# Attention scores as three float32r products on row halves, in an attention + MoE kernel

## The chip, the cores and the metric

The kernel runs on one core of a Trainium2 chip. The metric is the device time of one execution in microseconds. The engines are TensorE (PE, with its weight loads shown apart as PEld), VectorE (DVE), ScalarE (ACT), GpSimd (POOL) and SyncE (SP), which here issues the DMAs.

## The reference, cut to what matters

Attention with a learned bias by relative position comes first, with 4 batches, 8 heads, 576 tokens and 64 dimensions a head. Its output goes through a dense feed-forward layer (512 to 2048 to 512, 2304 tokens) and then a soft mixture of eight experts.

```python
scores = scale * np.matmul(q, k.transpose(0, 1, 3, 2))
...
h = np.maximum(x @ w1 + b1, 0.0)      # x: psi_rel / psi_i
bias = h @ w2
scores = scores + bias.transpose(2, 0, 1)[None, :, :, :]
scores = scores - np.max(scores, axis=-1, keepdims=True)
attn = np.exp(scores)
attn = attn / (np.sum(attn, axis=-1, keepdims=True) + 1e-09)
return np.matmul(attn, v).astype(np.float32)
...
h = x @ w_in
g = np.maximum(h, 0.0) + alpha * np.minimum(h, 0.0)
return (g @ w_out).astype(np.float32)
```

q and k are drawn large (factors 22 and 8), so the scores need nearly full float32.

## The kernel before, in words

**Stages.** The bias phase (0 to about 76 us) builds the bias with TensorE from masks that VectorE, ScalarE and GpSimd make, and stores its rows (`rows`) in a DRAM scratch `W`, from which the tiles `nb` are loaded. Attention follows (76 to about 395 us), then the feed-forward layer, called MoE in the code (to about 850), and the experts.

**Attention.** Work goes by 16 pairs: four head pairs `hp` times four batches. A pair has nine tiles of 128 query rows (`SLOT` gives their order; slots 0 to 3 and 5 to 8 are whole tiles of one head, slot 4 has the last 64 rows of both heads). `run` goes over the steps (pair i, tile t). A step issues:

- `scores` of the tile four steps ahead (L348): the 64 dimensions of a head stand twice in `raw`, on partitions 0 to 63 and 64 to 127, and each half multiplies the same queries with one half of the keys (288 columns), in float32. VectorE drains both halves from PSUM, adds the bias and takes the row's extreme (z and m, L353); ScalarE takes the exponential (e, L364).
- `transposes` of the tile of this step (L382): ten per tile, five chunks on either row half into two PSUM tiles, which ScalarE (L391) and VectorE (L393) copy into `g`.
- `sums` once a pair: reciprocals, and their transpose `tr` (L417), copied to `rt` (L419).
- `pv` (L402) when four or nine tiles are done: ten float32 matmuls of 256 or 320 columns into one PSUM tile `o`, which ScalarE copies to `xo` (L406) and a DMA stores in `xT`.

The input `raw` of a pair (q, k and v) is loaded two pairs ahead, in three buffers.

**Order.** The code order above is not the order on the engines: a planner moves instructions on their engine's queue, except those handed to `keep_in_program_order`. It decides from its own estimates, for instance, between which transposes a PV matmul stands, and where in VectorE's queue the MoE's first operations stand: `x_sum` (L504) multiplies loaded attention output (`xa` or `stage`) with its loaded row factors `rb`. Waits of DMAs are in SP's queue order: what SP's queue holds behind a waiting DMA waits too. `load_alpha` loads `nal` and lets GpSimd negate it.

PSUM holds two score tiles, three transpose tiles and one `o`. In the MoE, weights and activations are split in two float32r parts, and each product is three float32r products (`w0h`, `w0l`: the parts of the weights, the second made by GpSimd at L556).

Of the kernel before, what the change touches and what calls it, by code (L numbers as in the profile page):

```python
# [8 lines left out]
F32 = mybir.dt.float32  # L9
F32R = mybir.dt.float32r  # L10
# [3 lines left out]
AF = mybir.ActivationFunctionType  # L14
ALU = mybir.AluOpType
# [53 lines left out]
def bias_phase(tc, ident, W, cpack, lcol, prow, xmain, xtail, att):  # L69


    nc = tc.nc
    with ExitStack() as ctx:
# [162 lines left out]
        for k in range(NG):  # L236
            cs = [c for c in range(3, -1, -1) if k <= NG - 1 - c]
            if k < 5:
                cs.append(4)
            done = 0  # L240
            for n_, c in enumerate(cs):
                unit(k, c)
                if c in (2, 3) and k + c == 8:
                    att.bias_first(3 - c)
                if k + 1 < NG:
                    upto = 16 * (n_ + 1) // len(cs)
                    for u in range(done, upto):
# [9 lines left out]
class Attention:  # L257
# [7 lines left out]

    DONE = {3: 0, 8: 1}

    def __init__(self, tc, ident, W, xT, rs, qkv):
        self.tc, self.nc, self.ident = tc, tc.nc, ident
        self.W, self.xT, self.rs = W, xT, rs  # L270
        self.qkv = qkv
# [43 lines left out]
    def load(self, i):  # L315
        nc = self.nc
        hp, b = self.pairs[i]
        if b == 0 and hp > 0:
            self.bias_tile(hp)
            self.bias_rows(hp, 0, 4)  # L320
            self.bias_rows(hp, 4, 1)
        raw = self.rp.tile([P, 2368], F32, tag="raw", name=f"raw{i}")
        ins = nc.sync.dma_start(raw, self.qkv[hp, b])
        if i == 3:
            self.tc.keep_in_program_order(ins)
        self.st[i] = dict(
            hp=hp,
            b=b,
            i=i,
            q=raw[:, :1152].rearrange("p (h n) -> p h n", h=2),  # L330
            k=raw[:, 1152:1728].rearrange("p (h n) -> p h n", h=2),
            v=raw[:, 1728:].rearrange("p (h c d) -> p h c d", h=2, d=D),
        )

    def scores(self, i, t):
        nc, st = self.nc, self.st[i]
        slot = self.SLOT[t]
        if slot == 0:
            st["sum"] = self.op.tile([P, 9], F32, tag="sum", name=f"sum{i}")
        s = self.ps_s.tile([P, 2, 512], F32, tag="s", name=f"s{i}_{t}")  # L340
        if slot == 4:
            terms = [(64 * h, 64, h, 512) for h in range(2)]
        else:
            terms = [(0, P, slot // 5, P * (slot % 5))]
        for o, m_, h, r0 in terms:
            for hf in range(2):
                d = slice(64 * hf, 64 * hf + 64)
                nc.tensor.matmul(  # L348
                    s[o : o + m_, hf, :288], st["q"][d, h, r0 : r0 + m_], st["k"][d, h], start=True, stop=True
                )  # L350
        z = self.zp.tile([P, S], F32, tag="z", name=f"z{i}_{t}")
        m = self.zp.tile([P, 1], F32, tag="m", name=f"m{i}_{t}")
        nc.vector.tensor_tensor_reduce(  # L353
            out=z.rearrange("p (a b) -> p a b", a=2),
            in0=s[:, :, :288],
            in1=self.nb[st["hp"]][:, slot].rearrange("p (a b) -> p a b", a=2),
            scale=-0.125,
            scalar=3.0e38,
            op0=ALU.add,
            op1=ALU.min,  # L360
            accum_out=m,
        )
# [9 lines left out]
    def transposes(self, i, t):  # L372

        nc, st = self.nc, self.st[i]
        slot = self.SLOT[t]
        e = st.pop(("e", t))
        tp = [self.ps_t.tile([P, 5, 64], F32, tag="t", name=f"t{i}_{t}_{r}") for r in range(2)]
        for c in range(5):
            for r in range(2):
                q = slice(64 * r, 64 * r + 64)  # L380
                k0 = min(P * c, S - P)
                nc.tensor.transpose(tp[r][:, c], e[q, k0 : k0 + P], self.ident[q, q])  # L382
        for r in range(2):
            if slot == 4:
                dst = self.g_tile(st, r, 1)[:, :, 256:]
# [6 lines left out]
            else:  # L392
                nc.vector.tensor_copy(dst, tp[r])  # L393

    def pv(self, i, half):
        nc, st = self.nc, self.st[i]
        g = [st.pop(("g", h, half)) for h in range(2)]
        n = 320 if half else 256
        o = self.ps_o.tile([P, 320], F32, tag="o", name=f"o{i}_{half}")
        for c in range(5):  # L400
            for h in range(2):
                nc.tensor.matmul(  # L402
                    o[64 * h : 64 * h + 64, :n], st["v"][:, h, c], g[h][:, c, :n], start=c == 0, stop=c == 4
                )
        xo = self.op.tile([P, 320], F32, tag="xo", name=f"xo{i}_{half}")
        nc.scalar.activation(xo[:, :n], o[:, :n], AF.Copy)  # L406
        c0 = st["b"] * S + 256 * half
        nc.sync.dma_start(self.xT[st["hp"], :, c0 : c0 + n], xo[:, :n])

    def sums(self, i):  # L410
# [6 lines left out]
        nc.tensor.transpose(tp[:9], r, self.ident)  # L417
# [587 lines left out]

@with_exitstack
def kernel(
    ctx, tc, qkv, cpack, w_l, alpha, phi, mw1, mw2, lcol, prow, xmain, xtail, scon, out
):
    nc = tc.nc  # L1010
    dram = ctx.enter_context(tc.tile_pool(name="scratch", bufs=1, space=DRAM))
# [4 lines left out]
    ident = const.tile([P, P], F32, name="ident")  # L1016
    make_identity(nc, ident)

    att = Attention(tc, ident, W, xT, rs, qkv)
    att.open_set(ctx, 0)  # L1020
    rctx = ExitStack()
    att.rp = rctx.enter_context(tc.tile_pool(name="a_raw", bufs=3, reuse_waits="tile", side="right"))
# [107 lines left out]
def _layout(i):  # L1130
# [9 lines left out]
    parts = [np.stack([q, q], axis=2), kh, v_l]  # L1140
    qkv = np.concatenate([a.reshape(HP, B, P, -1) for a in parts], axis=3)
    wi = i["moe_w_in"].view(np.int64).reshape(NC, P, NF, P).transpose(2, 1, 0, 3).reshape(NF, P, NC * P)
    wo = i["moe_w_out"].view(np.int64).reshape(NF, P, DM)
    return dict(
        qkv=qkv,
        cpack=np.concatenate(
            [
                np.tile(i["w1"].reshape(HID, 1), (4, 1)),
# [41 lines left out]
```

## Time and profile before

| what | us |
|---|---|
| median of 3 runs | 934.61 (931.73 to 934.78) |
| the profiled execution | 929.26 |
| its span from first to last instruction | 927.4 |

| stage (us from the span's start) | what runs |
|---|---|
| 0 to 76 | bias phase |
| 76 to 395 | attention, 16 pairs |
| 395 to 850 | MoE |
| 850 to 927 | experts |

The profile is one execution. Its rows give an instruction group's source line, engine, operation, output and inputs with shapes and count; a float32 matmul leaves several records. "Idle before" is the time an engine stood still just before the group, with what released it. The granted clock is a share of full speed: 1.00 is 2.4 GHz, and 0.5 is 1.2 GHz.

### The profile page before, as it was taken

The page shows a single profiled execution, that of the slowest core. Times are in us where ns is not written, and L with a number is a line of the kernel's source. Part 1 is how long each engine was busy: PE and PEld are TensorE (multiplying, and loading weights), DVE is VectorE, ACT ScalarE, POOL GpSimd, SP SyncE. Part 2 cuts the span into 40 slices and gives each one's busy share as a digit, 9 for nine tenths or more (in the row PEclk, how much of TensorE's full clock was granted, in tenths as well). Part 3 has the DMA queues.
Part 4 walks back from the last instruction along what each step waited for, and adds up shares of the span by engine and source line. Part 5 has one row for each costly group of instructions (what it writes and reads, how often), then busy time and mean ns, then how long its engine had stood idle before and what let it go on. Part 6 is the DMA issues. An engine that isn't in the chain of part 4 may idle for free. (4 is left out here: it accounts for less than half of the span.)

```text
span 927.4 us, 17817 instructions
## 1 busy us (share of the span) xinstructions
PE 847.0 (91%) x7108; PEld 664.6 (72%) x7108; DVE 562.5 (61%) x1053; ACT 497.0 (54%) x1051; POOL 190.7 (21%) x141
## 2 busy tenths in 40 slices
PE   6787998899699899969999989998998999999894
PEld 6774665566466566659889978987987989888342
DVE  8865663665465566979963375576566666565202
ACT  8844665466365566534444565566655656555102
POOL 5851000000000000232222224234233224132100
PEclk9997999799799999979999999999998999999897
DMA  6898728136323530456520020032000003435995
GB/s 224 215 201 223 174 72 196 69 126 136 130 72 103 187 128 28 140 179 213 200 65 1 1 69 1 1 111 72 1 1 26 1 1 118 133 102 179 386 410 218
DMA packets 57186, 113.86 MB, mean 123 GB/s; under 512 B 10384, under 2 KB 37904, under 8 KB 53008
## 3 DMA queue, kind: packets, MB, share of 16 engines
q1 hardware_dynamic: 57104, 112.74, 39.2%
q8 instruction: 55, 0.90, 0.4%
q14 instruction: 27, 0.22, 0.1%
HBM read 91.43 MB, written 21.29 MB: 122 GB/s over the span
## 5 line engine op out<-in xcount | busy, mean ns | idle before, releaser
L348 PE MATMUL s<-raw 64*128 64x288 f32 (+1 forms) x640 | 124.9, 463 | 23.3 <-DVE m L353 21.0
L364 ACT ACTIVATE e<-z,m 128x576 f32<-128x576 f32 x144 | 111.1, 771 | 64.5 <-PE t L382 44.4
L353 DVE CUSTOM_DVE_ANT_0 z<-s,nb 128x576 f32<-128x576 f32 x144 | 106.7, 752 | 55.4 <-ACT g L391 29.3
L382 PEld LDWEIGHTS t<-ident,e 64*128 64x128 f32 x1440 | 99.3, 143 | 51.4 <-issue 14.6
L578 DVE SCALAR_TENSOR_TENSOR g<-g,nal 128x384 f32<-128x384 f32 x96 | 85.2, 887 | 81.3 <-ACT g L577 81.0
L382 PE MATMUL t<-ident,e 64*128 64x64 f32 x1440 | 111.4, 233 | 2.4 <-ACT g L391 1.1
L402 PE MATMUL o<-g,raw 128*64 128x256 f32 (+1 forms) x640 | 111.6, 416 | 0.6 <-DVE g L393 0.6
L585 ACT ACTIVATE gr<-g 128x384 fp32r<-128x384 f32 x95 | 49.8, 524 | 104.5 <-DVE g L578 104.5
L393 DVE COPY g<-t 128x320 f32<-128x320 f32 x144 | 68.5, 484 | 37.6 <-PE t L382 37.0
L348 PEld LDWEIGHTS s<-raw 64*128 64x128 f32 (+1 forms) x640 | 58.3, 185 | 43.2 <-DVE m L353 25.9
L391 ACT ACTIVATE g<-t 128x320 f32<-128x320 f32 x144 | 61.3, 428 | 35.1 <-PE t L382 33.9
L575 ACT ACTIVATE g<-h 128x384 f32<-128x384 f32 x96 | 46.8, 487 | 51.2 <-PE h L567 50.6
L160 PE MATMUL acc<-wp,mask 128*128 128x64 bf16 (+1 forms) x1680 | 56.1, 197 | 18.5 <-issue 10.9
L587 DVE TENSOR_TENSOR gr<-g,gr 128x384 fp32r<-128x384 f32 x79 | 52.6, 666 | 29.3 <-ACT gr L585 27.9
L160 PEld LDWEIGHTS <-mask 128*128 128x128 bf16 (+1 forms) x1680 | 54.1, 102 | 20.4 <-issue 13.5
L402 PEld LDWEIGHTS o<-g,raw 128*64 128x64 f32 x640 | 47.9, 136 | 28.6 <-DVE g L393 1.2
L556 POOL TENSOR_TENSOR w0l<-wr,w0h 128x1024 fp32r<-128x1024 f32 x1 | 2.4, 2369 | 284.5 <-ACT w0h L554 284.5
L141 ACT ACTIVATE mask<-pr,wb 128x576 bf16<-128x576 f16 (+4 forms) x81 | 46.8, 666 | 16.7 <-PE acc L160 16.7
L577 ACT ACTIVATE g<-h 128x384 f32<-128x384 f32 x96 | 46.6, 485 | 0.0
L587 POOL TENSOR_TENSOR gr<-g,gr 128x384 fp32r<-128x384 f32 x16 | 21.4, 1335 | 98.7 <-ACT gr L585 98.7
L504 DVE TENSOR_TENSOR xa<-xa,rb 128x384 f32<-128x384 f32 x12 | 11.6, 966 | 28.0 <-DMA xa<-xT 21.2
L534 DVE SCALAR_TENSOR_TENSOR wr<-stage,wr 128x1024 uint32<-128x1024 uint32 x16 | 28.2, 1765 | 0.3
(996 smaller groups left out, 1854.3 us busy)
## 6 DMA issues: line engine op xcount, KB each, us to landing
raw<-in_qkv_dram SPq DMA_DIRECT2D x16, 1184.0 KB
stage<-in_w_dram SPq DMA_DIRECT2D x16, 1024.0 KB
ep<-in_mw_dram SPq DMA_DIRECT2D x30, 512.0 KB
nb<-W SPq DMA_DIRECT2D x12, 576.0 KB
pre<-in_mw_dram SPq DMA_DIRECT2D x10, 512.0 KB
er<-in_mw_dram SPq DMA_DIRECT2D x9, 512.0 KB
em<-in_mw_dram SPq DMA_DIRECT2D x8, 512.0 KB
W<-rows SPq DMA_DIRECT2D x14, 256.0 KB
```

What stands on the lines that cost most here:

```text
L141: nc.scalar.activation(dst, pr[:, :n], AF.Sigmoid, bias=wb[:, t : t + 1], scale=BIG)
L160: nc.tensor.matmul(dst[:, u // 8, :, :, 4 * (u % 8) : 4 * (u % 8) + 4], mask[:, (16 * k + u) % RING, cols], wp[:, part], start=part == 0, ...
L348: nc.tensor.matmul(s[o : o + m_, hf, :288], st["q"][d, h, r0 : r0 + m_], st["k"][d, h], start=True, stop=True)
L353: nc.vector.tensor_tensor_reduce(out=z.rearrange("p (a b) -> p a b", a=2), in0=s[:, :, :288], in1=self.nb[st["hp"]][:, slot].rearrange("p ...
L364: nc.scalar.activation(e, z, AF.Exp, bias=m, scale=-1.0, accum_out=st["sum"][:, slot : slot + 1])
L382: nc.tensor.transpose(tp[r][:, c], e[q, k0 : k0 + P], self.ident[q, q])
L391: nc.scalar.activation(dst, tp[r], AF.Copy)
L393: nc.vector.tensor_copy(dst, tp[r])
L402: nc.tensor.matmul(o[64 * h : 64 * h + 64, :n], st["v"][:, h, c], g[h][:, c, :n], start=c == 0, stop=c == 4)
L578: nc.vector.scalar_tensor_tensor(g, neg, self.nal[:, f : f + 1], g, ALU.mult, ALU.add)
L585: nc.scalar.activation(gh, g, AF.Copy)
L587: eng.tensor_tensor(gl, g, gh.bitcast(F32), ALU.subtract)
```

## The change

The scores use float32r: GpSimd splits q and k of a pair into a high part (a copy to float32r) and the rest (a difference), each tile's score is `kh*qh + kl*qh + kh*ql`, accumulated in PSUM, again with the key columns halved over the two row halves. Slot 4 no longer uses quarter tiles: the host pads its queries with zero columns, so that the two heads are six products that add up in one tile. `raw` has only q and k now (two buffers), v has its own tile and DMA (three buffers). The parts of pair 0 and 1 are made in the bias phase and ahead of the first scores, those of later pairs during the pair before.

Scores, transposes, row-sum transposes and PV matmuls of all pairs but the first are kept in program order. PV of a half is issued in two runs, chunks 0 to 2 in one step and chunks 3 and 4 in the next, and `xo` is copied by VectorE.

```diff
+            if k < 4:
+                att.split(0, k)
...
-        raw = self.rp.tile([P, 2368], F32, tag="raw", name=f"raw{i}")
-        ins = nc.sync.dma_start(raw, self.qkv[hp, b])
-        if i == 3:
+        raw = self.rp.tile([P, 1792], F32, tag="raw", name=f"raw{i}")
+        nc.sync.dma_start(raw, self.qk[hp, b])
+        v = self.vp.tile([P, 2, 5, D], F32, tag="v", name=f"v{i}")
+        nc.sync.dma_start(v, self.v_l[hp, b])
+        self.st[i] = dict(hp=hp, b=b, i=i, raw=raw, v=v)
+
+    def split(self, i, k):
+
+        st = self.st[i]
+        x = "qk"[k // 2]
+        src = st["raw"][:, :1216] if x == "q" else st["raw"][:, 1216:]
+        if k % 2 == 0:
+            st[x, 0], st[x, 1] = (
+                self.sp.tile([P, src.shape[1]], F32R, tag=x + "hl"[n], name=f"{x}{'hl'[n]}{i}") for n in range(2)
+            )
+            self.nc.gpsimd.tensor_scalar(st[x, 0], src, 1.0, 1.0, ALU.mult, ALU.mult)
+        else:
+            self.nc.gpsimd.tensor_tensor(st[x, 1], src, st[x, 0].bitcast(F32), ALU.subtract)
+
+    def pin(self, i, ins):
+
+        if i > 0:
             self.tc.keep_in_program_order(ins)
...
-        if slot == 4:
-            terms = [(64 * h, 64, h, 512) for h in range(2)]
+        if slot < 4:
+            terms = [(P * slot, 0)]
+        elif slot == 4:
+            terms = [(512, 0), (576, 1)]
         else:
-            terms = [(0, P, slot // 5, P * (slot % 5))]
-        for o, m_, h, r0 in terms:
+            terms = [(704 + P * (slot - 5), 1)]
+        seq = [(o, h, a, b) for o, h in terms for a, b in ((0, 0), (0, 1), (1, 0))]
+        for n_, (o, h, a, b) in enumerate(seq):
             for hf in range(2):
                 d = slice(64 * hf, 64 * hf + 64)
-                nc.tensor.matmul(
-                    s[o : o + m_, hf, :288], st["q"][d, h, r0 : r0 + m_], st["k"][d, h], start=True, stop=True
+                self.pin(
+                    i,
+                    nc.tensor.matmul(
+                        s[:, hf, :288],
+                        st["q", a][d, o : o + P],
+                        st["k", b][d, 288 * h : 288 * h + 288],
+                        start=n_ == 0,
+                        stop=n_ == len(seq) - 1,
+                    ),
                 )
...
-                nc.tensor.transpose(tp[r][:, c], e[q, k0 : k0 + P], self.ident[q, q])
+                self.pin(i, nc.tensor.transpose(tp[r][:, c], e[q, k0 : k0 + P], self.ident[q, q]))
...
-    def pv(self, i, half):
+    def pv(self, i, half, chunks):
...
-        o = self.ps_o.tile([P, 320], F32, tag="o", name=f"o{i}_{half}")
-        for c in range(5):
+        if chunks[0] == 0:
+            st["o"] = self.ps_o.tile([P, 320], F32, tag="o", name=f"o{i}_{half}")
+        o = st["o"]
+        for c in chunks:
...
-        nc.scalar.activation(xo[:, :n], o[:, :n], AF.Copy)
+        nc.vector.tensor_copy(xo[:, :n], o[:, :n])
...
+        for k in range(4):
+            self.split(1, k)
...
-                pend.append(lambda i=i1, half=self.DONE[t1]: self.pv(i, half))
+                pend += [lambda i=i1, half=self.DONE[t1], c=c: self.pv(i, half, c) for c in ((0, 1, 2), (3, 4))]
+            if t < 4 and 0 < i < np_ - 1:
+                self.split(i + 1, t)
...
+    att.rp, att.vp, att.sp = (
+        rctx.enter_context(tc.tile_pool(name=n, bufs=b, reuse_waits="tile", side="right"))
+        for n, b in (("a_raw", 2), ("a_v", 3), ("a_split", 2))
+    )
```

The order on TensorE in pair 5, before: `s6_3` are the scores of pair 6's tile 3, `t5_4_0` the transposes of tile 4 into the first of its two PSUM tiles, `o5_0` the PV of pair 5's first half.

```order
L348 MATMUL s6_3_3701<-raw6_3326 128x288 x2
L382 MATMUL t5_4_0_3604<-ident_63,e5_4_3483 128x64 x5
L402 MATMUL o5_0_3643<-g5_0_0_3497,raw5_3080 64x256
L382 MATMUL t5_4_1_3605<-ident_63,e5_4_3483 128x64 x5
L382 MATMUL t5_5_0_3628<-ident_63,e5_5_3517 128x64 x5
L402 MATMUL o5_0_3643<-g5_1_0_3531,raw5_3080 64x256
```

The same half in the changed order (the second of its two runs):

```order
L405 MATMUL t5_6_0_3984<-ident_63,e5_6_3853 128x64
L405 MATMUL t5_6_1_3985<-ident_63,e5_6_3853 128x64
L429 MATMUL o5_0_3965<-g5_0_0_3785,v5_3289 64x256
L429 MATMUL o5_0_3965<-g5_1_0_3826,v5_3289 64x256
L429 MATMUL o5_0_3965<-g5_0_0_3785,v5_3289 64x256
L429 MATMUL o5_0_3965<-g5_1_0_3826,v5_3289 64x256
L366 MATMUL s6_2_4005<-kh6_3876,qh6_3799 128x288 x2
L366 MATMUL s6_2_4005<-kl6_3877,qh6_3799 128x288 x2
L366 MATMUL s6_2_4005<-kh6_3876,ql6_3800 128x288 x2
```

One PV matmul no longer stands alone between transposes, and the transposes of the two row halves alternate.

The order on VectorE at the end of pair 3, before: `xa3_0` is an input of the MoE's block 3.

```order
L393 COPY g3_1_1_3148<-t3_8_1_3218 128x5x64
L504 TENSOR_TENSOR xa3_0_7615<-xa3_0_7615,rb3_0_7616 128x384
L353 ISA z4_6_3307,m4_6_3308<-s4_6_3302,nb1_2827 128x576
L353 ISA m4_6_3308 128x1
L353 ISA z4_7_3331,m4_7_3332<-s4_7_3328,nb1_2827 128x576
```

The same place in the changed order:

```order
L416 COPY g3_1_1_3370<-t3_8_1_3452 128x5x64
L376 ISA z4_4_3472,m4_4_3473<-s4_4_3465,nb1_2984 128x576
L376 ISA m4_4_3473 128x1
L416 COPY g4_0_0_3489<-t4_0_1_3478 128x5x64
```

And where `xa3_0` now stands, in pair 15 (`wr1`, `wr2` are weights of the MoE that VectorE narrows):

```order
L444 TENSOR_SCALAR r15_7020<-sum15_6642 128x9
L538 TENSOR_TENSOR xa3_0_8423<-xa3_0_8423,rb3_0_8424 128x384
L569 SCALAR_TENSOR_TENSOR wr1_6908<-stage_5891,wr1_6908 128x1024
```

The operation moved from pair 3 to pair 15; `xa3_1` moved likewise from pair 7, since the DMA of `rb3_0` now waits for a late split buffer's memory.

SP's queue at the end of the bias phase, before (W stores, loads of `nb0`, and `nal`):

```order
L303 DMA nb0_1641<-W_57 64x2x576 x4
L198 DMA W_57<-rows2_2_1699 64x6x128 x2
L198 DMA W_57<-rows0_2_1518 64x6x192 x2
L198 DMA W_57<-rows1_3_1935 64x6x128 x2
L198 DMA W_57<-rows0_3_2118 64x6x128 x2
L485 DMA nal_5001<-in_alpha_dram 128x16
```

And in the changed order:

```order
L198 DMA W_57<-rows1_3_1951 64x2x128
L519 DMA nal_5592<-in_alpha_dram 128x16
L198 DMA W_57<-rows2_2_1715 64x2x128
L305 DMA nb0_1657<-W_57 64x2x576
L198 DMA W_57<-rows0_2_1534 64x2x192
L305 DMA nb0_1657<-W_57 64x2x576
```

`nal` moved ahead of W stores and of loads of `nb0`; on GpSimd its negation moved ahead of the last two `rows` copies.

## Rows read from the trace of the kernel before

**Rows 1.** The page's first part: busy time, share of the span, instructions.

```profile
PE 847.0 (91%) x7108; PEld 664.6 (72%) x7108; DVE 562.5 (61%) x1053; ACT 497.0 (54%) x1051; POOL 190.7 (21%) x141
```

**Rows 2.** Transposes by window: length, PE and PEld busy (count), clock, DMA; L417's starts.

```profile
156.00:182.50 26.50, 8.51 (x92) 7.87 (x90) 0.81 0.41 111
182.50:199.90 17.40, 6.13 (x90) 5.51 (x90) 1.00 0.26 88
...
217.60:245.40 27.80, 6.67 (x90) 6.06 (x90) 0.82 0.68 165
...
297.70:319.60 21.90, 7.91 (x90) 6.88 (x90) 0.92 0.67 226
...
L417 PE MATMUL tr<-ident,r x16: 273/278/278, 102.3 to 390.2; 128*9 128x128 f32 x16
```

**Rows 3.** A clean window: us, PE, PEld, DVE, ACT, POOL busy, clock, DMA share, GB/s.

```profile
172.00:229.00 57.00, 57.00 (x563) 36.58 (x560) 35.63 (x103) 36.33 (x94) 0.00 (x0) 1.00 0.37 101
```

**Rows 4.** Waits of VectorE, 80 to 420 us: total us, times, longest.

```profile
DVE xa L504 <- DMA xa<-xT: 19.5, 2, 9.8
...
DVE stage L504 <- DMA stage<-rs: 5.8, 2, 3.5
```

**Rows 5.** Timeline after the first long wait: start, us, instruction, [idle before, releaser].

```profile
165.42 1.32 PE L348 MATMUL s<-raw 64*128 64x288 f32 x2 [6.27 <-DVE m L353]
```

**Rows 6.** Timeline of TensorE in a clean pair.

```profile
190.78 0.51 PEld L382 LDWEIGHTS t<-ident,e 64*128 64x128 f32 x10 [0.39 <-ACT g L391]
190.78 0.64 PE L382 MATMUL t<-ident,e 64*128 64x64 f32 x10
...
191.36 1.95 PE L402 MATMUL o<-g,raw 128*64 128x256 f32 x16
...
193.23 0.53 PE L382 MATMUL t<-ident,e 64*128 64x64 f32 x5
...
193.69 0.65 PE L402 MATMUL o<-g,raw 128*64 128x256 f32 x2
...
194.26 0.76 PE L348 MATMUL s<-raw 64*128 64x288 f32 x4
...
194.85 0.47 PE L382 MATMUL t<-ident,e 64*128 64x64 f32 x9
```

**Rows 7.** Timeline of TensorE in the MoE: float32r products and a load.

```profile
500.69 0.19 PEld L567 LDWEIGHTS h<-x,w12l 128*128 128x128 f32 x1
...
501.04 0.51 PE L567 MATMUL h<-x,w11h 128*128 128x384 f32 x2
...
501.56 0.51 PE L567 MATMUL h<-x,w11h 128*128 128x384 f32 x2
```

**Rows 8.** ScalarE: back-to-back steps in the timeline, and its PV copies by line.

```profile
197.34 0.78 ACT L364 ACTIVATE e<-z,m 128x576 f32<-128x576 f32 x1 [0.46 <-ACT g L391]
...
198.44 0.76 ACT L364 ACTIVATE e<-z,m 128x576 f32<-128x576 f32 x1
...
L406 ACT ACTIVATE xo<-o 128x320 f32<-128x320 f32 (+1 forms) x30 | 12.1, 404 | 21.7 <-PE o L402 20.8
```

**Rows 9.** Groups of GpSimd: busy us, mean ns, idle before.

```profile
L193 POOL TENSOR_SCALAR rows<-rows 128x512 f32<-128x512 f32 x28 | 17.1, 620 | 17.7 <-DVE rows L185 17.7
L556 POOL TENSOR_TENSOR w0l<-wr,w0h 128x1024 fp32r<-128x1024 f32 x1 | 2.4, 2369 | 284.5 <-ACT w0h L554 284.5
L587 POOL TENSOR_TENSOR gr<-g,gr 128x384 fp32r<-128x384 f32 x16 | 21.4, 1335 | 98.7 <-ACT gr L585 98.7
```

**Rows 10.** The start: timeline rows, and a window (columns as in rows 3).

```profile
54.16 0.62 POOL L193 TENSOR_SCALAR rows<-rows 128x512 f32<-128x512 f32 x1 [7.61 <-DVE rows L185]
...
86.26 0.76 DVE L353 CUSTOM_DVE_ANT_0 z<-s,nb 128x576 f32<-128x576 f32 x1 [3.80 <-DMA nb<-W]
...
95.37 0.21 POOL L486 TENSOR_SCALAR nal<-nal 128x16 f32<-128x16 f32 x1 [17.33 <-DMA nal<-in_alpha_dram]
...
50.00:60.00 10.00, 9.57 (x273) 9.25 (x271) 7.22 (x13) 5.24 (x11) 5.84 (x8) 0.88 1.11 203
```

More of the change, by code (lines that the diff above doesn't have):

```diff
@@ L266, with __init__ @@
     DONE = {3: 0, 8: 1}
-    def __init__(self, tc, ident, W, xT, rs, qkv):
+    def __init__(self, tc, ident, W, xT, rs, qk, v_l):
         self.tc, self.nc, self.ident = tc, tc.nc, ident
         self.W, self.xT, self.rs = W, xT, rs
-        self.qkv = qkv
+        self.qk, self.v_l = qk, v_l
         self.pairs = [(hp, b) for hp in range(HP) for b in range(B)]
@@ L321, in load @@
             self.bias_rows(hp, 4, 1)
-        raw = self.rp.tile([P, 2368], F32, tag="raw", name=f"raw{i}")
-        ins = nc.sync.dma_start(raw, self.qkv[hp, b])
-        if i == 3:
-            self.tc.keep_in_program_order(ins)
[L326 to L333, printed above, removed]
+        raw = self.rp.tile([P, 1792], F32, tag="raw", name=f"raw{i}")
[16 more added lines that the diff above has]
+        if i > 0:
+            self.tc.keep_in_program_order(ins)
     def scores(self, i, t):
@@ L393, in transposes @@
                 nc.vector.tensor_copy(dst, tp[r])
-    def pv(self, i, half):
+    def pv(self, i, half, chunks):
         nc, st = self.nc, self.st[i]
-        g = [st.pop(("g", h, half)) for h in range(2)]
         n = 320 if half else 256
-        o = self.ps_o.tile([P, 320], F32, tag="o", name=f"o{i}_{half}")
-        for c in range(5):
+        if chunks[0] == 0:
+            st["o"] = self.ps_o.tile([P, 320], F32, tag="o", name=f"o{i}_{half}")
+        o = st["o"]
+        for c in chunks:
             for h in range(2):
-                nc.tensor.matmul(
-                    o[64 * h : 64 * h + 64, :n], st["v"][:, h, c], g[h][:, c, :n], start=c == 0, stop=c == 4
-                )
+                g = st["g", h, half]
+                self.pin(
+                    i,
+                    nc.tensor.matmul(
+                        o[64 * h : 64 * h + 64, :n], st["v"][:, h, c], g[:, c, :n], start=c == 0, stop=c == 4
+                    ),
+                )
+        if chunks[-1] < 4:
+            return
         xo = self.op.tile([P, 320], F32, tag="xo", name=f"xo{i}_{half}")
-        nc.scalar.activation(xo[:, :n], o[:, :n], AF.Copy)
+        nc.vector.tensor_copy(xo[:, :n], o[:, :n])
         c0 = st["b"] * S + 256 * half
@@ L416, in sums @@
         tp = self.ps_t.tile([P, P], F32, tag="t", name=f"tr{i}")
-        nc.tensor.transpose(tp[:9], r, self.ident)
+        self.pin(i, nc.tensor.transpose(tp[:9], r, self.ident))
         rt = self.op.tile([9, P], F32, tag="rt", name=f"rt{i}")
@@ L1007 @@
 def kernel(
-    ctx, tc, qkv, cpack, w_l, alpha, phi, mw1, mw2, lcol, prow, xmain, xtail, scon, out
+    ctx, tc, qk, v_l, cpack, w_l, alpha, phi, mw1, mw2, lcol, prow, xmain, xtail, scon, out
 ):
@@ L1017 @@
     make_identity(nc, ident)
-    att = Attention(tc, ident, W, xT, rs, qkv)
+    att = Attention(tc, ident, W, xT, rs, qk, v_l)
     att.open_set(ctx, 0)
     rctx = ExitStack()
-    att.rp = rctx.enter_context(tc.tile_pool(name="a_raw", bufs=3, reuse_waits="tile", side="right"))
+    att.rp, att.vp, att.sp = (
+        rctx.enter_context(tc.tile_pool(name=n, bufs=b, reuse_waits="tile", side="right"))
+        for n, b in (("a_raw", 2), ("a_v", 3), ("a_split", 2))
+    )
     bias_phase(tc, ident, W, cpack, lcol, prow, xmain, xtail, att)
@@ L1139, in _layout @@
     v_l[:, :, 64:, :, 4] = v[:, :, :, 512:].transpose(0, 1, 3, 2, 4)
-    parts = [np.stack([q, q], axis=2), kh, v_l]
-    qkv = np.concatenate([a.reshape(HP, B, P, -1) for a in parts], axis=3)
+    q_l = np.zeros((HP, B, 2, D, 1216), i["q"].dtype)
+    q_l[..., :576] = q[:, :, None, :, 0, :]
+    q_l[..., 640:704] = q[:, :, None, :, 1, 512:]
+    q_l[..., 704:] = q[:, :, None, :, 1, :512]
+    qk = np.concatenate([q_l.reshape(HP, B, P, 1216), kh.reshape(HP, B, P, S)], axis=3)
     wi = i["moe_w_in"].view(np.int64).reshape(NC, P, NF, P).transpose(2, 1, 0, 3).reshape(NF, P, NC * P)
@@ L1144, in _layout @@
     return dict(
-        qkv=qkv,
+        qk=qk,
+        v_l=v_l.reshape(HP, B, P, 2, 5, D),
         cpack=np.concatenate(
```

## The prediction

> **What bounds the kernel now.** I read the page first, then the stages, then the waits inside the attention stage, and last single steps.
>
> The first part of the page shows TensorE busy 91% of 927.4 us [rows 1]. The change touches attention only, so its worth has to be read there. Attention runs from about 76 to 395 us as 16 pairs of nine steps, and each pair leaves 90 transposes in the records. [rows 2] shows pairs by that count: 17.4 us where nothing disturbs, and 26.5, 27.8 and 21.9 us in three others. The row-sum transpose, one a pair, runs from 102.3 to 390.2 [rows 2]; less the three long ones that leaves 211.7 us for twelve pairs, 17.6 each. In a window with the clock at 1.00 (2.4 GHz) TensorE is busy 57.00 of 57.00 us [rows 3], so a clean pair is TensorE's own work plus what it loses between runs of unlike instructions.
>
> The two long pairs have one cause. VectorE waits 9.8 us twice for the DMA that brings `xa`, an input of the first MoE that nobody needs for a long time [rows 4]. The operation stands in VectorE's queue ahead of the score drains z; TensorE then waits for z, 6.3 us from the last matmul's modelled end [rows 5], and its clock over those two pairs is 0.81 and 0.82 [rows 2]. So two costs are on the path: 17.6 us a pair of TensorE, and 26.5 + 27.8 - 2 x 17.6 = 19 us of the two waits with what the slow clock adds.
>
> **Scores.** Before, a tile is four records of fp32 (two on each row half) and takes 194.26 to 194.85, 0.59 us [rows 6]; slot 4's, in eight smaller records, I take as equal. A pair has nine: 5.3 us. After, a tile is three fp32r products on both row halves. The rate of one fp32r product is in the MoE's rows: three products of 384 columns from 501.04 to 501.56, 0.173 us each [rows 7], so 288 columns take 0.13 and three 0.39, if the two halves run side by side as the fp32 halves do. Entry and exit: PV's sixteen records of 256 columns took 1.87 us [rows 6], two at a time 0.234, or 0.26 for 288 columns; the fp32 tile's 0.59 less two of these leaves 0.06. I take 0.09, since three products cross more weight changes: 0.48 a tile, 0.87 for slot 4, whose products are six (it now uses zero-padded columns instead of quarter tiles). A pair: 8 x 0.48 + 0.87 = 4.7 us. The arithmetic alone saves only 0.6 us a pair, 9 us in fifteen pairs.
>
> **Order on TensorE.** The larger part comes from what stands next to what. Before, the planner puts a lone PV matmul between transposes: its two records cost 0.57 us (193.69 to 194.26), while sixteen in one run cost 1.87, so one more pair of records in a run costs (1.87 - 0.57) / 7 = 0.19 [rows 6]. After, each half's PV comes in two runs, of 12 and 8 records: 0.57 + 5 x 0.19 = 1.5 and 0.57 + 3 x 0.19 = 1.1; half 1 has 320 columns, 5/4 of that: 1.9 and 1.4. That is 5.9 us a pair; the entries of the longer half grow less than its columns, so I take 5.6. Transposes: ten in one run cost 0.58 ahead of PV (190.78 to 191.36), five, one half only, cost 0.46 ahead of a PV piece [rows 6]; before, most stand in fives. After, all stand in tens: 4 x 0.58 + 5 x 0.45 = 4.6. Together 10.2 us, where a clean pair before, less its scores and the row-sum transpose of 0.28 [rows 2], leaves 17.6 - 5.3 - 0.3 = 12.0. TensorE's sum after is 4.7 + 10.2 + 0.3 = 15.2 us.
>
> What is late next: in the five steps without PV TensorE needs 0.48 + 0.45 = 0.93 us, and ScalarE's e and g copy take 1.10 when they run back to back (197.34 to 198.44) [rows 8]; the strict order leaves little to average over, since the transposes of a step wait for the previous step's g copy. That adds 5 x 0.17, some of it again for latencies: 0.6 to 1.6. VectorE gets the two PV copies that ScalarE loses (0.40 us each) [rows 8]; its step is z and a copy, start to start about 1.2 us, its pair 9 x 1.2 + 0.8 + 0.7 = 12.3, under the pair. I take **15.8 us a pair**, 1.8 less: 15 x 1.8 = **27 us**. Ends: 15.2 (36 us) and 16.8 (12 us).
>
> **The two waits.** In the changed order `xa3_0` and `xa3_1` stand in the last pair, where their data has long landed, because the rows that they need are now loaded into memory that a late split buffer frees. Both waits go: **19 us**. The waits of block 0's `stage` (the longest 3.5 us) [rows 4] stay where they were.
>
> **GpSimd's parts.** New work, idle engine: ahead of `w0l`, its first operation for the MoE, it waits 284.5 us [rows 9]. A copy of 512 columns takes 0.62 us, a difference of 1024 takes 2.4 [rows 9]. A pair: copies of 1216 and 576 columns 1.5 + 0.7, differences 2.8 + 1.3, sum 6.3 us, against 15.8. Where VectorE works beside it, a 384-column difference takes 1.34 on the mean (3.5 ns a column) [rows 9], which makes 8.4. It is hidden with room, and if it took twice as long it still would be. VectorE's z and copies read PSUM; I add nothing for them, and they have 3 us of room a pair.
>
> **Start.** Three prices, overlapping. (1) GpSimd makes the parts of pairs 0 and 1 during the bias phase, 12.6 us, of which its idle stretch ahead of 54.16 (7.6 us) takes more than half [rows 10]. (2) SP loads one more pair early (about 1 MB) among the W stores, where the DMA share is already 1.11 at 203 GB/s [rows 10]: up to 1 MB / 203 GB/s = 5 us. (3) The load of `nal` now stands ahead of W stores and of `nb0`, waits for the last bias matmul, and GpSimd's `nal`, with the last two `rows` copies behind it, waits for its landing (17.3 us of idle GpSimd, to 95.37, before); z waits 3.8 us for `nb` already [rows 10]. I take **+5 us**, between 0 (the first scores wait elsewhere) and +10.
>
> **Sum.** Against the profiled execution of 929.26 us: -27 - 19 + 5 = -41, 888 us. The runs' median of 934.61 stands 5.3 us above that execution; carrying this over gives **893 us**. Its own ends: -36 - 19 = -55 gives 880, less some 4 us of `stage` waits if they go too, 876; -12 - 19 + 10 = -21 gives 914.
>
> **Rivals.**
>
> *Program order costs as many waits as the interleaving did.* A TensorE that may not run ahead waits for e, g copy and z in turn; only the score arithmetic's 0.6 us a pair stays: -9 - 19 + 5 = -23, 912 us. For it: ScalarE's 1.10 is already above 0.93. Against: the nearness is in five of nine steps, and PV fills the other four.
>
> *Weight loads set the pace of the scores.* Each product brings a new weight on each half. If a load hides behind no matmul shorter than itself, the MoE's 128-column load of 0.19 us [rows 7] replaces 0.13: tile 0.65, +1.5 us a pair, of which 0.3 fall into ScalarE's slack: 15 x 1.2 = +18, 912 us. Against: ten 128-column loads of transposes start within one run of 0.51 us [rows 6]. The Trainium skill ("TensorE: Matmul & The Clock Gate", section on LDWEIGHTS) gives a load as its columns over 1.2 in ns, 107 ns for 128; six in a row would be an estimated 0.64 us a tile, the same outcome. The transposes' row, 0.05 a load, disagrees with it.
>
> *The waits move instead of going.* Another load's consumer is drawn into VectorE's queue early and waits as `xa` did: -27 + 5 = -22, 913 us. Against: the order shows no such operation between the z of pairs 1 to 11.
>
> *The slower side: fp32r products of the two row halves run one after the other.* Place: every score tile. Six products of 0.13 and entry are 0.87 us a tile, 1.65 in slot 4, 8.6 us of scores a pair: +3.9, less 0.7 of ScalarE's slack, so 19.0 us a pair, +1.4 over before: 15.5 pairs x 1.4 = +22, with -19 + 5 this is +8, 943 us. It turns slower once a pair passes 17.6 + 14/15.5 = 18.5 us, a tile 0.8. For it: no row shows two fp32r halves at work. Against: the fp32 halves of a tile, four records in 0.59 us, do share the array.
>
> *The change doesn't do what it says* (products not at fp32r's rate): excluded nearly, since the order shows the products with fp32r tiles and the MoE's rows show that rate.
>
> **Chances.** Forecast 0.56, program order 0.15, loads 0.07, waits moved 0.07, a start of +15 us or more (some 904) 0.03, halves in turn 0.09, a half-way of that which ends within 0.3% 0.03. About 0.3% is what a measurement of this kernel can tell from no change. Faster 0.88, same 0.03, slower 0.09. The range 873 to 916 takes in the forecast's ends and the rivals of 904 to 913, and leaves out the slower rival, its half-way and a little below.
>
> **What would show it.** Score tiles: six records within 0.5 us, halves starting together; 0.9 would be the slower rival, 0.65 the loads. PV in four runs a pair without lone records, transposes in tens. The pairs' spacing at 15 to 17 us with no pair of 26; the list of VectorE's waits without `xa` in attention, `stage` kept. GpSimd busy some 100 us more and never waited for by a score, except at the start. First z later than before by some us, `nal` ahead. A spacing near 17 with TensorE idle behind ScalarE would be the program-order rival. I would be wrong most simply if a wait that I don't see, at the start or where SP's queue waits for GpSimd, holds the first pairs.

## The result, and the profile after

The changed kernel takes 906.13 us, the median of four runs (900.49 to 911.04), against 934.37 before; the ratio is 0.970 (95% interval 0.964 to 0.976). A later set of six runs beside the kernel before gave 0.968 (0.966 to 0.971). Forecast were 893 us and 873 to 916: the sign and the range held, the gain was 28 us instead of 41.

The profiled execution has a span of 898.7 us, 28.7 less than before. The starts of the row-sum transposes, one a pair, cut it in three. Before, the first stood at 102.3 us and the last at 390.2 [rows 2]; the line's row in the changed kernel:

```profile
L447 PE MATMUL tr<-ident,r x16: 277/278/385, 111.2 to 368.1; 128*9 128x128 f32 x16
```

| part of the span | before | after | difference |
|---|---|---|---|
| to the first row-sum transpose | 102.3 | 111.2 | +8.9 |
| from the first to the last (15 pairs) | 287.9 | 256.9 | -31.0 |
| from the last to the end | 537.2 | 530.7 | -6.5 |

The pairs one by one, as in [rows 2] (one clean pair, then the last seven): window, its length, the transposes' PE and PEld busy time with counts, granted clock, DMA share, GB/s.

```profile
143.63:159.55 15.92, 5.44 (x93) 4.46 (x90) 1.00 0.52 140
...
240.88:258.05 17.17, 5.56 (x91) 4.67 (x90) 0.91 0.29 80
258.05:273.97 15.92, 5.46 (x93) 4.46 (x90) 1.00 0.33 97
273.97:291.67 17.70, 5.72 (x93) 4.52 (x90) 1.00 0.58 206
291.67:314.30 22.63, 6.13 (x93) 4.76 (x90) 0.85 0.34 108
314.30:332.94 18.64, 6.24 (x93) 5.06 (x90) 0.91 0.22 61
332.94:349.75 16.81, 5.56 (x91) 4.66 (x90) 0.90 0.06 19
349.75:368.05 18.30, 4.82 (x83) 3.80 (x80) 0.97 0.30 102
```

A clean pair is 15.9 us, where it was 17.6, and no pair of 26 us is left. But the last five pairs, which made 92.5 us before (4.5 over five clean ones of 17.6), make 94.1 now, 14.5 over five clean ones of 15.9.

Inside a clean pair the timeline shows something that no row of before had (start, duration, engine, line, instruction; weight loads and accumulator reads left out):

```profile
168.32 2.79 POOL L341 TENSOR_TENSOR ql<-raw,qh 128x1216 fp32r<-128x1216 f32 x1
168.43 1.51 PE L429 MATMUL o<-g,v 128*64 128x256 f32 x12
...
168.76 2.38 DVE L444 TENSOR_SCALAR r<-sum 128x9 f32<-128x9 f32 x1
...
170.38 0.47 PE L405 MATMUL t<-ident,e 64*128 64x64 f32 x10
170.78 1.08 PE L429 MATMUL o<-g,v 128*64 128x256 f32 x8
...
171.05 0.48 DVE L416 COPY g<-t 128x320 f32<-128x320 f32 x1
...
171.79 0.40 PE L366 MATMUL s<-kh,qh 64*128 64x288 f32 x2
...
172.30 0.47 PE L405 MATMUL t<-ident,e 64*128 64x64 f32 x10
```

TensorE does what was forecast: a score tile from 171.79 to 172.30, 0.51 us (0.48 forecast); transposes in tens, 0.40 (0.45 to 0.58); PV in runs of 12 and 8, the second 1.01 us (1.1). VectorE doesn't. Its addition of 1e-9 to nine row sums takes 2.38 us and ends with GpSimd's difference. By line, with shortest, median and longest duration in ns, of the changed kernel and of the kernel before:

```profile
L444 DVE TENSOR_SCALAR r<-sum x16: 161/2370/2393, 102.4 to 363.7; 128x9 f32<-128x9 f32 x16
```

```profile
L414 DVE TENSOR_SCALAR r<-sum x16: 159/169/173, 94.8 to 383.4; 128x9 f32<-128x9 f32 x16
```

In 13 of the 16 pairs the difference of 1216 columns runs beside it; it then takes 2.2 to 2.4 us and ends each time 0.03 us behind the difference. In the three pairs where GpSimd is idle it takes 0.16 to 0.17. It waits for GpSimd, and it stands in the middle of VectorE's queue. The Trainium skill ("SBUF — State Buffer", section "Who interferes with whom") states this: a VectorE tensor_scalar in a mode that uses both of its ports, or an operation with two SBUF inputs beside a GpSimd read, is blocked for the whole GpSimd instruction when GpSimd issued first. These rows agree; which mode the addition ran in, no row shows.

### The profile page after: what moved, and what is told of

Same layout as the page of the kernel before. It is cut to its first block, busy times and chain, and to the rows that moved or that the text cites. A ratio compares the mean times of both kernels' runs of the same rounds, so it can differ in the third digit from the quotient of the medians.

```text
span 898.7 us, 18451 instructions
## 1 busy us (share of the span) xinstructions
PE 813.7 (91%) x7428; PEld 655.7 (73%) x7428; DVE 604.0 (67%) x1085; ACT 487.1 (54%) x1019; POOL 288.7 (32%) x205
## 4 chain that ended last, share of the span: by engine, by line
PE 60%; DVE 19%; DMA 9%; ACT 4%; issue 4%; POOL 1%; SPq 1%; DVEq 0%; ACTq 0%; POOLq 0%
PE ys L633 17%; PE h L601 16%; PE o L429 6%; PE acc L160 5%; DVE z L376 4%; PE s L366 4%; DMA xT<-xo 3%; PE ops L1005 2%; PE t L405 2%; DVE r L444 2%; PE hps L1005 2%; DVE g L416 2%; DMA stage<-in_w_dram 2%; DMA W<-rows 1%; ACT e L387 1%
## 5 line engine op out<-in xcount | busy, mean ns | idle before, releaser
L612 DVE SCALAR_TENSOR_TENSOR g<-g,nal 128x384 f32<-128x384 f32 x96 | 90.7, 945 | 78.6 <-ACT g L611 78.3
L387 ACT ACTIVATE e<-z,m 128x576 f32<-128x576 f32 x144 | 111.2, 772 | 45.0 <-DVE m L376 43.4
L405 PE MATMUL t<-ident,e 64*128 64x64 f32 x1440 | 92.5, 235 | 24.2 <-ACT g L414 19.3
L405 PEld LDWEIGHTS t<-ident,e 64*128 64x128 f32 x1440 | 76.2, 144 | 39.8 <-ACT g L414 32.8
L429 PE MATMUL o<-g,v 128*64 128x256 f32 (+1 forms) x640 | 100.4, 437 | 0.3 <-DVE g L416 0.3
L160 PE MATMUL acc<-wp,mask 128*128 128x64 bf16 (+1 forms) x1680 | 59.7, 202 | 18.2 <-issue 10.9
L366 PE MATMUL s<-kh,qh 64*128 64x288 f32 x320 | 66.2, 394 | 10.3 <-DVE rows L185 6.6
L339 POOL TENSOR_SCALAR qh<-raw 128x1216 fp32r<-128x1216 f32 x16 | 19.5, 1218 | 161.3 <-PE s L366 157.7
L366 PEld LDWEIGHTS s<-kh,qh 64*128 64x128 f32 x320 | 34.5, 197 | 41.2 <-issue 21.5
L429 PEld LDWEIGHTS o<-g,v 128*64 128x64 f32 x640 | 43.4, 144 | 28.2 <-issue 5.3
L366 PE MATMUL s<-kl,qh 64*128 64x288 f32 x320 | 51.8, 306 | 0.0
L366 PE MATMUL s<-kh,ql 64*128 64x288 f32 x320 | 51.5, 305 | 0.0
L621 POOL TENSOR_TENSOR gr<-g,gr 128x384 fp32r<-128x384 f32 x16 | 22.6, 1416 | 85.9 <-ACT gr L619 85.9
```

What stands on the lines that cost most here:

```text
L160: nc.tensor.matmul(dst[:, u // 8, :, :, 4 * (u % 8) : 4 * (u % 8) + 4], mask[:, (16 * k + u) % RING, cols], wp[:, part], start=part == 0, ...
L366: nc.tensor.matmul(s[:, hf, :288], st["q", a][d, o : o + P], st["k", b][d, 288 * h : 288 * h + 288], start=n_ == 0, stop=n_ == len(seq) - 1,),
L405: self.pin(i, nc.tensor.transpose(tp[r][:, c], e[q, k0 : k0 + P], self.ident[q, q]))
L429: nc.tensor.matmul(o[64 * h : 64 * h + 64, :n], st["v"][:, h, c], g[:, c, :n], start=c == 0, stop=c == 4),
L612: nc.vector.scalar_tensor_tensor(g, neg, self.nal[:, f : f + 1], g, ALU.mult, ALU.add)
L621: eng.tensor_tensor(gl, g, gh.bitcast(F32), ALU.subtract)
```

## The experiments

All ratios are to the kernel before on the same chip and in the same set of runs. The pair lengths come from the profiles.

**The addition left out.** The reciprocal is taken straight from the sums.

```diff
-        nc.vector.tensor_scalar(r, st["sum"], 1e-9, None, ALU.add)
-        nc.vector.reciprocal(r, r)
+        nc.vector.reciprocal(r, st["sum"])
```

> The changed kernel with the row sums' reciprocal taken straight from the sums, without the VectorE addition of 1e-9 (which the sums, at least 1, do not feel in float32). In the trace of the changed kernel that addition of 9 columns takes 2.37 us in 13 of 16 pairs, each time beside GpSimd's difference of 1216 columns, and 0.17 us in the three pairs without it. Theory A (VectorE is shut out by GpSimd for that time, and it is on the path): pairs fall from 15.9 to about 15.3 us, with fewer waits of transposes for g copies; 13 x 0.6 = 8 us, so about 898 against 906. Rival B (the 2.2 us of VectorE is in its slack): pairs stay at 15.9 and the time within 2 us of 906.

Measured: 0.965 (0.960 to 0.971). A clean pair of this run, 0.4 us shorter than in the changed kernel:

```profile
170.66:186.18 15.52, 5.46 (x93) 4.46 (x90) 1.00 0.29 80
```

The wait for GpSimd is on the path, for 0.4 of its 2.2 us a pair; 0.6 was expected. By its time alone the run isn't told from the changed kernel, since the intervals overlap; the pairs show it.

The reciprocal now stands where the addition stood, beside the same difference in 13 pairs, with its operands in SBUF too, and it isn't held up:

```profile
L444 DVE RECIPROCAL r<-sum x16: 202/210/216, 100.2 to 357.6; 128x9 f32<-128x9 f32 x16
```

So not every small VectorE operation on SBUF waits for GpSimd; the kind of operation decides.

**The waits for `xa` alone.** In the kernel before, the multiplication of `xa` for block 3, chunks 0 and 1, is kept in program order on VectorE, which puts it behind attention.

```diff
-        self.nc.vector.tensor_tensor(xu, xu, rb, ALU.mult)
+        i = self.nc.vector.tensor_tensor(xu, xu, rb, ALU.mult)
+        if pin:  # blk == 3 and c < 2
+            self.tc.keep_in_program_order(i)
```

> The kernel before with one thing alone: the operations on xa of block 3, chunks 0 and 1, are kept in program order on VectorE, so that they leave attention. Theory A (the two waits cost what the two long pairs show): 19 us less, about 915 of 934. Rival B (they hide other waits that then show): at most 12 us less, 922 or more.

Measured: 0.987 (0.980 to 0.993), 12 us by the ratio, 14 by the medians of 915.4 and 929.4. In its profile the first long pair falls from 26.5 to 17.6 us, the second only from 27.8 to 21.2, with 19.1 behind it:

```profile
157.04:174.62 17.58, 7.09 (x92) 6.30 (x90) 1.00 0.62 166
...
209.72:230.93 21.21, 6.36 (x90) 5.67 (x90) 0.99 0.84 202
230.93:250.00 19.07, 7.03 (x91) 6.34 (x90) 0.92 0.25 86
```

There TensorE waits 3.3 us for a `raw` load instead. The waits are worth 19 us only where nothing else is late behind them.

**The order alone.** The kernel before with float32 scores, but with the changed kernel's program order, two PV runs a half and PV's copy on VectorE.

```diff
+    def pin(self, i, ins):
+        if i > 0:
+            self.tc.keep_in_program_order(ins)
...
-                pend.append(lambda i=i1, half=self.DONE[t1]: self.pv(i, half))
+                pend += [lambda i=i1, half=self.DONE[t1], c=c: self.pv(i, half, c) for c in ((0, 1, 2), (3, 4))]
```

> The kernel before with float32 scores and one raw tile, but scores, transposes and PV in program order, PV in two runs a half, and PV's copy on VectorE. The waits for xa stay in attention here. Theory A (order gives most of the pair's 1.7 us): TensorE's sum is 0.6 us a pair over the changed kernel's, so pairs of about 16.4 us, 15 x 1.1 = 17 us less than before, about 917. Rival B (the arithmetic gives most): pairs of 17 to 17.6, 925 to 934.

Measured: 0.978 (0.973 to 0.983), 906.9 us, with both waits for `xa` still there:

```profile
151.40:178.15 26.75, 5.77 (x93) 4.65 (x90) 0.81 0.49 127
178.15:193.74 15.59, 5.30 (x93) 4.42 (x90) 1.00 0.29 99
...
224.91:252.98 28.07, 5.76 (x93) 4.65 (x90) 0.82 0.48 121
```

Both theories undersold it. Float32 scores in this order make pairs of 15.59 us, shorter than the changed kernel's 15.9 and within 0.08 of the run without the addition. "The order" is three edits here (program order, PV in two runs, PV's copy on VectorE), which were not run singly in float32.

**The scores alone.** The changed kernel with `pin` doing nothing, so that the planner orders TensorE.

```diff
     def pin(self, i, ins):
-        if i > 0:
-            self.tc.keep_in_program_order(ins)
+        pass
```

> The changed kernel without program order: the planner places scores, transposes and PV (still in two parts a half) as it likes. Theory A (order gives most): pairs of about 17 us, 16 us more than the changed kernel, about 922. Rival B (arithmetic gives most): pairs of 16 to 16.4, within 8 us of 906.

Measured: 0.985 (0.978 to 0.991), 912.3 us, clean pairs of 16.83 to 16.88 us. A clean pair, and two of the last five:

```profile
174.88:191.75 16.87, 7.92 (x90) 6.97 (x90) 1.00 0.30 93
...
276.05:298.43 22.38, 8.26 (x90) 7.29 (x90) 0.90 0.60 193
...
318.21:340.19 21.98, 6.17 (x90) 5.55 (x90) 0.92 0.17 50
```

Program order alone thus brings 1.0 us a pair to the float32r scores (16.9 to 15.9). The 0.7 us that is left to the kernel before belongs to the three products, to PV in two runs and to its copy on VectorE together, less the addition's wait; it isn't split further. With float32 scores the three edits of order brought 2.0, so the gains of order and arithmetic don't add.

The last five pairs take 101.3 us here, 17.0 over five clean ones, although nothing is kept in order on TensorE.

**Order and late `xa`, float32 scores.** The run with the order alone, and `xa` kept late.

> The kernel before, float32 scores, with program order, PV in two runs and PV's copy on VectorE (as in the run with the order alone), and the xa operations kept late. Theory A (the two gains add): the order alone took 22 us and the late xa alone 14, so some 33 to 38 us under the kernel before, ratio 0.96; at or below the changed kernel without the addition. Rival B (with xa gone other waits come into its place): ratio 0.97 or more.

Measured: 889.5 us, 0.955 (0.952 to 0.957). Theory A: the two gains add, 41 us by the medians, even a little more than the sum of 22 and 14 (in this order the two long pairs are 23.6 us over clean ones). This kernel has no float32r score, and by the ratios it is 1.4% faster than the changed one in the same set (0.968).

**One product instead of three.** Without the addition, and with the high parts' product alone; the two correcting products are left out.

```diff
-        seq = [(o, h, a, b) for o, h in terms for a, b in ((0, 0), (0, 1), (1, 0))]
+        seq = [(o, h, a, b) for o, h in terms for a, b in ((0, 0),)]
```

> The kernel without the addition of 1e-9, and with one product (high parts) a score tile instead of three; the two correcting products are left out, so a third of the scores' matmuls remains. TensorE has 2 x 0.13 x 10 = 2.6 us less a pair. Theory A (pairs of 15.5 us are set by ScalarE's e and g copies and their waits in the five steps without PV): pairs fall by at most 1.2 us, the four PV steps' share. Rival B (TensorE sets them): pairs fall by 2.3 us or more, to about 13.

Measured: 0.941 (0.938 to 0.945). Its pairs:

```profile
166.92:181.10 14.18, 5.57 (x93) 4.39 (x90) 1.00 0.37 110
181.10:196.93 15.83, 5.58 (x93) 4.38 (x90) 0.89 0.31 101
```

Taking 2.6 us of matmuls from TensorE shortens a clean pair by 1.3, half of it, near theory A's 1.2. Most of the other half is TensorE's waits for ScalarE's g copies (total us, times, longest). In the clean pair of the run without the addition (170.66 to 186.18), and in one of this run (166.92 to 181.10):

```profile
PE t L405 <- ACT g L414: 0.7, 2, 0.4
```

```profile
PE t L405 <- ACT g L414: 1.7, 4, 0.6
```

In the run without the addition ScalarE runs e, g, e, g without a gap in the steps without PV, and so does VectorE with z and its copy:

```profile
169.74 0.41 ACT L414 ACTIVATE g<-t 128x320 f32<-128x320 f32 x1
170.06 0.76 ACT L387 ACTIVATE e<-z,m 128x576 f32<-128x576 f32 x1
...
170.82 0.42 ACT L414 ACTIVATE g<-t 128x320 f32<-128x320 f32 x1
171.14 0.77 ACT L387 ACTIVATE e<-z,m 128x576 f32<-128x576 f32 x1
```

```profile
169.19 0.75 DVE L376 CUSTOM_DVE_ANT_0 z<-s,nb 128x576 f32<-128x576 f32 x1
...
169.87 0.49 DVE L416 COPY g<-t 128x320 f32<-128x320 f32 x1
170.27 0.75 DVE L376 CUSTOM_DVE_ANT_0 z<-s,nb 128x576 f32<-128x576 f32 x1
```

A step is 1.08 us there on both (170.06 to 171.14, 169.19 to 170.27), and each e starts within about 0.1 us of the end of its z. A faster score tile changes nothing in either. Which of the two sets the pace, these rows don't tell, and no run relieved one of them alone; theory A's "set by ScalarE" is shown only as "not set by TensorE".

**The loads of `raw` 2 and 3 late.** Without the addition; these loads are kept in program order and so leave the W stores.

```diff
-        nc.sync.dma_start(raw, self.qk[hp, b])
+        ins = nc.sync.dma_start(raw, self.qk[hp, b])
+        if i in (2, 3):
+            self.tc.keep_in_program_order(ins)
```

> The kernel without the addition, with the loads of raw 2 and 3 kept in program order, so that they leave the bias phase's W stores (1.8 MB later). Theory A (the early loads hold up the stores and so the first scores): first scores at 76 to 79 us instead of 83 to 85, 4 to 6 us less than without this edit. Rival B (GpSimd's parts in the bias phase hold it up): no change in the first scores, and the time within 2 us, or worse where GpSimd waits for the late loads.

Measured: 0.963 (0.961 to 0.965), as without the edit. First scores at 83.6 us, against 83.0 without it: rival B, as far as the loads go.

**The changed kernel again.**

> The changed kernel once more, unedited, on this chip beside the others: 0.970 of the kernel before, within the interval of the result; its first scores tell how much the start varies between executions (84.6 us in the profiled one).

Measured: 0.968 (0.966 to 0.971), first scores at 83.0, first row-sum transpose at 110.5.

**Pairs 0 and 1 in float32.** Without the addition; their scores read `raw`, so GpSimd makes no parts in the bias phase.

```diff
+        if i < 2:
+            seq = [(o, h, None, None) for o, h in terms]
...
-            if k < 4:
-                att.split(0, k)
...
-        for k in range(4):
-            self.split(1, k)
```

> The kernel without the addition, with the scores of pairs 0 and 1 in float32 from raw, so that GpSimd makes no parts in the bias phase (and the loads of raw 2 and 3 come late by themselves); nal stands ahead of W stores as in the changed kernel. Theory A (GpSimd's 12 us of parts hold up the bias phase): first scores back at 76 to 78 us, the first row-sum transpose at 103 instead of 107 to 111, and some 5 us less than without this edit. Rival B (nal's place, or a start that varies by itself): first scores at 82 us or later.

Measured: 0.972 (0.967 to 0.976), so nothing gained, but it shows the mechanism. First scores at 75.6 us (before 76.1, changed 84.6) and the first row-sum transpose at 102.8: GpSimd's parts held up the bias phase. `nal` still stands ahead of W stores in SP's queue here, but on GpSimd no copy of `rows` stands behind its negation any more, so its price isn't separated by this run. The 8 us come back at once: the planner now loads `raw` 2 behind the W stores, GpSimd waits for it, and the next pair takes 26 us:

```profile
113.29 1.21 POOL L337 TENSOR_SCALAR qh<-raw 128x1216 fp32r<-128x1216 f32 x1 [31.21 <-DMA raw<-in_qk_dram]
```

**The loads of block 0 spaced.** The float32 kernel in order with late `xa`; each of the four inputs of the MoE's block 0 is loaded four steps before its multiplication, which is kept behind the score drain of that step.

```diff
-XHOOK = ((-4, 7), (-3, 0), (-3, 5), (-3, 8))
+XHOOK = ((-4, 0), (-4, 4), (-4, 8), (-3, 3), (-3, 7))
...
-        at(*XHOOK[c], x_first, c)
+        if c:
+            at(*XHOOK[c], x_first, c - 1, moe.x_make)
+        at(*XHOOK[c], x_first, c, moe.x_load)
+    at(*XHOOK[HP], x_first, HP - 1, moe.x_make)
```

> Float32 scores in program order with late xa, and the loads of block 0's four inputs spaced by four steps, each input's multiplication kept on VectorE behind the scores' drain four steps later. Theory A (the five late pairs lose 13 us over 15.6 each because VectorE's queue stands behind these loads): they come down to 15.6 to 16.5, 8 to 12 us less than without the edit, some 880. Rival B (the weights' narrowing and other work make them long): at most 4 us less.

Measured: 881.3 us, 0.944 (0.940 to 0.948), the fastest that computes all. The last five pairs fall from 91.2 to 85.1 us, and two of them are clean:

```profile
262.30:277.89 15.59, 5.30 (x93) 4.42 (x90) 1.00 0.59 184
277.89:293.48 15.59, 5.30 (x93) 4.43 (x90) 1.00 0.57 197
293.48:310.50 17.02, 5.27 (x93) 4.29 (x90) 1.00 0.42 138
310.50:328.39 17.89, 5.73 (x93) 4.62 (x90) 0.90 0.05 18
328.39:347.38 18.99, 5.01 (x83) 3.69 (x80) 1.00 0.40 124
```

Theory A's mechanism holds, at 6 us in the pairs instead of 8 to 12; VectorE's list of waits there has no `stage` load left. The last three pairs keep 7 us over clean ones. I did not separate their causes.

**The same with float32r scores.** Pairs 0 and 1 in float32, no addition, and the spacing.

> The same spacing with float32r scores (pairs 0 and 1 in float32, no addition of 1e-9). Theory A (the three products bring nothing once the order is kept): within 4 us of the float32 kernel with the spacing, on either side. Rival B (they bring the 0.1 us a tile that TensorE saves): 8 us less or more.

Measured: 898.7 us, 0.963 (0.959 to 0.967), 17 us behind the float32 kernel: outside both theories. Clean pairs are 15.50 us against 15.59, as theory A says. The two profiled spans are 18.7 us apart: 10.9 in the pair behind the first (28.0 us, as above, against 17.1), 5.7 in the other pairs, some with the clock down, and 6.5 behind attention, less 4.3 ahead of the first row-sum transpose. What makes the part behind attention wasn't tried. Two of these pairs:

```profile
100.58:128.56 27.98, 5.64 (x93) 4.88 (x90) 0.76 0.51 130
...
240.86:257.39 16.53, 5.55 (x91) 4.66 (x90) 0.92 0.28 81
```

Against the run with pairs 0 and 1 in float32, of which this one is the spaced form, the spacing works in float32r too: the last five pairs fall from 94.9 to 86.7 us. Their second, in that run and in this one:

```profile
290.55:313.78 23.23, 5.89 (x91) 4.89 (x90) 0.83 0.31 101
```

```profile
288.41:305.32 16.91, 5.72 (x93) 4.52 (x90) 1.00 0.49 174
```

## Why the prediction was right or wrong

**The clean pair (15.8 forecast, 15.9 measured): right in size, wrong in make-up.** The order was rightly named the larger part. The step that failed is the credit of 0.6 us a pair to the score arithmetic. The sum counted it in full on TensorE and then put ScalarE's floor on top as a small addition. The runs show 0.08 us: 15.59 with float32 and 15.51 with three float32r products in the same order. In the five steps without PV ScalarE and VectorE run without a gap at 1.08 us, and what a tile saves on TensorE there is lost. The prediction held ScalarE against TensorE step by step, but VectorE only by the pair (12.3 us), though its own figure for VectorE's step, 1.2, was the longest of the three. On TensorE, too, the credit was nearer 0.4: eight tiles at 0.51 against 0.59, but slot 4 at 0.90 (173.70 to 174.60 without the addition) against 0.65 in float32 (181.19 to 181.84 with the order alone), where the prediction took 0.87 and 0.59. The rival "program order costs as many waits" named waits that are there, and its price was wrong: fifteen pairs of 17.0 didn't come.

**VectorE beside GpSimd: the step "I add nothing for them" failed.** It looked at z and the copies, which read PSUM and indeed kept their 0.75 and 0.48 us. It left out the addition, whose operands are all in SBUF, 2.2 us longer in 13 pairs, 0.4 us a pair on the path: some 5 us in all.

**The two waits (19 us): right.** Two pairs of 26 and 28 us became clean. Alone they gave 12 to 14 us in the planner's order, and some 19 us in program order (22 and 41 us under the kernel before of the two sets).

**The sentence "the waits of block 0's `stage` stay where they were": failed, at some 10 us.** They stayed in place, but they cost TensorE more. The last five pairs were 4.5 us over clean ones before and 14.5 after, although VectorE's own waits for these loads fell from 10.9 to 6.3 us; TensorE's waits there rose from 4.7 to 13.8. With float32 scores the edits of order do this by themselves: 14.6 us over clean pairs in the run with the order alone. Program order isn't the whole cause, since float32r scores in the planner's order are 17.0 over; what makes them so stays open. That the loads have a large part in it is shown by the spacing, which took 6 us off in float32 and 8 in float32r. The granted clock is 0.85 and 0.91 over the pairs of 22.6 and 18.6 us. In the longest, VectorE's multiplication waits for the load and then for GpSimd, and TensorE waits for a copy queued behind it:

```profile
301.67 2.74 POOL L341 TENSOR_TENSOR ql<-raw,qh 128x1216 fp32r<-128x1216 f32 x1
302.72 2.10 DVE L538 TENSOR_TENSOR stage<-stage 128x384 f32<-128x384 f32 x1 [2.12 <-DMA stage<-xT]
...
305.28 1.27 PE L405 MATMUL t<-ident,e 64*128 64x64 f32 x10 [3.87 <-DVE g L416]
```

The rival "the waits move instead of going" looked for a new early operation; what happened is that an old wait got dearer for TensorE.

**The start (+5 forecast, +8.9 measured).** Inside its bounds of 0 to 10. Of the three prices the first, GpSimd's parts, is the one: without them the first scores are back at 75.6 us. Late loads alone changed nothing at the first scores. `nal` wasn't moved alone; by the rows its part is small. In the changed kernel the last drains of the bias phase wait for a W store, and the first scores for those drains; `nal` on GpSimd, with two copies of `rows` behind it, comes after the drains began, and VectorE waits 0.9 us for those copies, at the first z:

```profile
83.72 1.29 DVE L185 TENSOR_TENSOR rows<-tmp,acc 128x512 f32<-128x512 f32 x2 [4.56 <-DMA W<-rows]
...
84.19 0.20 POOL L520 TENSOR_SCALAR nal<-nal 128x16 f32<-128x16 f32 x1 [5.13 <-DMA nal<-in_alpha_dram]
84.50 1.22 POOL L193 TENSOR_SCALAR rows<-rows 128x512 f32<-128x512 f32 x2
...
84.56 0.61 PE L366 MATMUL s<-kh,qh 64*128 64x288 f32 x2 [6.64 <-DVE rows L185]
```

**Behind attention (-6.5 us, not forecast).** The planner places the MoE's first operations anew with each edit. From the last row-sum transpose to the end the kernels took 527.9 to 539.1 us (537.2 before). Before, TensorE had one stop of 5.85 us in the first blocks of the MoE; the changed kernel's longest there is 2.6. What makes the rest of the spread wasn't tried.

**The sum.** Pairs 15 x (15.9 - 17.6) = -25 and the waits -19, against forecasts of -27 and -19. Then +9 at the start instead of +5, +13 in pairs that are no longer clean (10 of it in the last five) instead of 0, and -6.5 behind attention instead of 0: -29 instead of -41.

**The slower rival** (row halves in turn) is out: three products on two halves take 0.51 us. So is the rival of weight loads, which asked 0.65. Six loads one after the other by the Trainium skill's rule ("TensorE: Matmul & The Clock Gate", section on LDWEIGHTS), an estimated 0.64 us, are not what the tile shows.

## What to carry to other kernels

Before counting what a faster instruction saves, ask for each step which engine ends it; here ScalarE and VectorE fill five of nine steps, and 0.1 us a tile saved on TensorE came to 0.08 us a pair. When a change does several things, run each alone: here the order and a moved wait carried all of the gain, the named arithmetic carried almost none, and leaving it out gave a faster kernel (889.5 against 900.8 us in one set; with the loads spaced 881.3 against 898.7 in another). When work goes to an idle GpSimd, list the VectorE operations whose operands are all in SBUF, and look at each in a trace: here an addition and a multiplication waited for GpSimd and a reciprocal didn't. When an engine is put in strict order, price again every DMA wait that stands in its partners' queues.

## What the runs showed that I had not expected

- A VectorE operation on nine columns took 2.37 us beside a GpSimd difference of 1216 columns, and 0.17 without it; a multiplication of 384 columns took 2.10 instead of 0.56; a reciprocal of nine columns kept its 0.21.
- With the least work on TensorE its clock fell most often. In float32 the order's clean stretches stay at 1.00. The changed kernel has a pair at 0.91 (240.88 to 258.05), in and ahead of which TensorE never stood longer than 0.7 us; in its second profile the same pair is clean. With one product a tile three pairs of the first nine are at 0.89 and 15.8 us instead of 14.2, and the mean clock of its two executions is 0.948 and 0.949, against 0.958 to 0.960 in the four executions without the addition. The level in such a stretch is half, 1.2 GHz. That the lighter work is the cause wasn't tried.

```profile
240.05:255.96 15.91, 5.46 (x90) 4.46 (x90) 1.00 0.30 90
```
